# Block mixing with the data stationary: keys and values mixed straight into transposed form, Sinkhorn without matmuls, scores of two heads at once

## The chip, the cores and the metric

The kernel runs on one core of one Trainium2 chip. The metric is the device time of one execution in microseconds (us), as a median over several runs. Most executions of one kernel agree within a fraction of a per cent.

The engines are named as in the profile. PE is TensorE (matmuls), PEld its weight loads, DVE is VectorE, ACT is ScalarE, POOL is GpSimd and SP is SyncE. SBUF is the on-chip memory from which the engines work. PSUM is the small memory into which TensorE writes, and from which VectorE and ScalarE copy the results out. Such a copy is called an eviction here.

## The reference

There are 4 batches, 8 heads, 768 tokens in 8 blocks of 96, and a head width of 64. Each head has an 8x8 matrix, which is normalised and then mixes the blocks of keys and values. Attention is local to a block. A token mix and a two-layer channel MLP follow.

```python
P = sort_net                                   # [4, 8, 8, 8]
for _ in range(5):                             # Sinkhorn
    P = np.exp(P - np.max(P, axis=-1, keepdims=True))
    P = P / (np.sum(P, axis=-1, keepdims=True) + 1e-09)
    P = P / (np.sum(P, axis=-2, keepdims=True) + 1e-09)
k_sorted = np.einsum('bhij,bhjcd->bhicd', P, k_b)   # k_b: [4, 8, 8 blocks, 96, 64]
v_sorted = np.einsum('bhij,bhjcd->bhicd', P, v_b)
scores = scale * q_b @ k_sorted.T                   # per block, 96 x 96
x = softmax(scores) @ v_sorted                      # then [4, 768, 512]
a1 = alpha1 * x + beta1
u  = x + lam * np.einsum('ts,bsd->btd', w_tok, a1)  # token mix, 768 x 768
a2 = alpha2 * u + beta2
out = u + lam * (np.maximum(a2 @ w_ch1, 0.0) @ w_ch2)   # 512 -> 2048 -> 512
```

## The kernel before

Mixing works on a pair of batches: 2 batches x 8 heads x 8 blocks are 128 rows, so one 128x128 block-diagonal matrix (`bigP2`) mixes them all. The matrix is stationary and the data are moving, so each result comes out as it went in: rows are blocks, and a block's 96 tokens lie along the row. Attention needs tokens on the partitions. The kernel gets there by writing the mixed rows to DRAM and reading them back.

```python
def do_mix(bp):
    for (src, kv) in ((k, 0), (v, 1)):
        # ... for half, for chn: load raw [128, 1024]
        for n in range(2):
            mx = psb([128, 512], FT, name="mix_ps")
            nc.tensor.matmul(mx[:], bigP2[bp][:], raw[:, n * 512:(n + 1) * 512], start=True, stop=True)
            nc.scalar.copy(sort_t[:, chn * 1024 + n * 512: chn * 1024 + (n + 1) * 512], mx[:])
        # ... then, per batch, the DRAM scratch
        nc.sync.dma_start(kvscr[bb][:, :, kv, :]...[:, half * 48:(half + 1) * 48, :], sort_t[...]...)

def head_stage1(b, h):                              # one head at a time
    # ... the Q tile, and the tile kvn with its ones
    nc.sync.dma_start(kvn[:, :, 0:2 * D], kvscr[b, h].rearrange("(i t) kv d -> t i (kv d)", t=BLK))
    # ... the PSUM tile kTps
    for i in range(NB):                             # K once more, turned on TensorE
        nc.tensor.transpose(kTps[:, i * BLK:(i + 1) * BLK], kvn[:, i, 0:D], ident16[0:BLK, 0:BLK])
    # ... the SBUF tile kTs
    nc.vector.tensor_copy(kTs[:], kTps[:])
    # ... eight 96x96 score matmuls, exp on ScalarE
```

Other parts that the change touches are these. Sinkhorn uses ones-vector matmuls for its sums. 32 small DMAs put its result into `bigP2`. The attention output goes through a second DRAM scratch (`xscr`), to come back in token tiles. The affine of the channel MLP is folded into W1, with 64 bias matmuls. TensorE does not run the parts strictly in the order in which the program writes them: in this trace matmuls of the channel MLP (line 255) stand between those of an attention (lines 150, 163 and 181).

The softmax here doesn't subtract the row's maximum and nothing guards it: scores larger than these inputs give would overflow.

## Time and profile before

| | before |
|---|---|
| time, median | 434.53 us (434.02 to 438.99, the 3 runs before the prediction) |
| TensorE busy | 330.0 us of 433.1 |
| DRAM scratch and other small moves (queue q1) | 77,880 packets, 12.60 MB |
| from 180 us on | TensorE busy nearly all of every stretch |

The first view is the page of the profile. A strip has 40 slices of the span, and each digit is the busy share in tenths. A group line reads: source line, engine, operation, output<-input, shapes, count, then busy us and mean ns of one, then how long the engine stood idle just before them and on what.

```profile
span 433.1 us, 5706 instructions
...
PE   2474204432588342999999999999999999999996
...
ACT  1040004332334110177720066740046780048600
...
q1 hardware_dynamic: 77880, 12.60, 17.3%
...
L127 ACT CAST sort<-mix_ps 128x512 f16<-128x512 f32 x48 | 24.8, 605 | 63.4 <-DMA kvscr<-sort 22.0
...
L150 PE MATMUL kT_ps<-ident_71,kvn 96*64 96x96 f16 x256 | 19.4, 227 | 1.7 <-DMA kvn<-kvscr 1.7
```

The second view is the table by stretches of the same kernel: the stretch, its length, busy us of PE, PEld, DVE, ACT and POOL, then the clock granted to TensorE, the DMA share and GB/s.

```profile
60.00:80.00 20.00, 7.14 (x14) 1.17 (x14) 0.00 (x0) 6.25 (x12) 7.48 (x15) 1.00 0.62 90
80.00:100.00 20.00, 6.94 (x13) 1.08 (x14) 0.00 (x0) 6.07 (x12) 3.70 (x7) 1.00 1.17 183
...
180.00:200.00 20.00, 19.76 (x205) 13.55 (x203) 8.42 (x28) 13.50 (x29) 0.00 (x0) 1.00 0.18 41
200.00:220.00 20.00, 20.00 (x174) 12.81 (x174) 6.37 (x25) 15.18 (x28) 3.28 (x4) 1.00 0.85 174
```

There are two regimes. Up to 180 us every engine is mostly idle: in the mixing (60 to 100 us) TensorE works a third of the time, and ScalarE, which evicts 128x512 tiles at 605 ns each, waits 22.0 us in all for its tile to be stored to the scratch. From 180 us on TensorE is the bound. The change aims at the first regime, and takes some TensorE work (the 256 K transposes of line 150) out of the second.

### The profile page before, as it was taken

To read this page: it belongs to the slowest core of one execution; us is meant where nothing else is said; L and a number is where in the kernel's file an instruction comes from. 1 tells how busy PE (TensorE), PEld (TensorE's weight loads), DVE (VectorE), ACT (ScalarE), POOL (GpSimd) and SP (SyncE) were. 2 spreads that over 40 slices of the span, in tenths; PEclk is the share of its full clock that TensorE was granted. 3 is DMA by queue.
4 is the path that set the end of the run, shared out by engine and by line. 5 is a ranking of instruction groups with operands and counts; after the bars stand their busy time and mean duration, and the time that the engine had idled before them with its cause. 6 is when DMAs were issued, how large, how long until landed. Compare 5 with 4: busy or idle time off the path is not lost.

```text
span 433.1 us, 5706 instructions
## 1 busy us (share of the span) xinstructions
PE 330.0 (76%) x2264; PEld 182.0 (42%) x2264; DVE 156.4 (36%) x375; ACT 147.6 (34%) x290; POOL 64.8 (15%) x109
## 2 busy tenths in 40 slices
PE   2474204432588342999999999999999999999996
PEld 1331000000275230466644566654456654456542
DVE  0459830000144324545363435419335517330011
ACT  1040004332334110177720066740046780048600
POOL 6737142121100240000300030030010000000000
PEclk9999999999999996899999999999999999999999
DMA  9999706999967999413942173491221153300012
GB/s 87 157 211 202 89 0 101 183 173 158 200 121 115 188 66 233 68 38 76 180 124 87 40 45 74 112 209 50 98 18 38 38 144 108 113 2 0 2 73 74
DMA packets 120658, 44.30 MB, mean 102 GB/s; under 512 B 104824, under 2 KB 110712, under 8 KB 120632
## 3 DMA queue, kind: packets, MB, share of 16 engines
q0 software_dynamic: 35984, 21.90, 34.9%
q1 hardware_dynamic: 77880, 12.60, 17.3%
q10 hardware_dynamic: 6768, 9.44, 6.5%
q8 instruction: 18, 0.29, 0.3%
q14 instruction: 8, 0.07, 0.0%
HBM read 39.86 MB, written 15.73 MB: 128 GB/s over the span
## 4 chain that ended last, share of the span: by engine, by line
issue 45%; PE 27%; DMA 17%; DVE 5%; POOL 3%; ACTq 2%; ACT 0%; POOLq 0%; DVEq 0%
PE ch_ps L268 10%; PE h_ps L255 9%; DMA raw<-in_k_dram 4%; DMA raw<-in_v_dram 4%; DMA W1p_96<-in_moe_w_ch_dram 3%; DMA qn_1204<-in_q_dram 2%; ACTq L345 2%; PE tok_ps L226 2%; DVE jsum_r L324 2%; DMA qn_128<-in_q_dram 1%; DMA qn_172<-in_q_dram 1%; PE qT_ps L102 1%; PE x_ps L181 1%; PE mix_ps L122 1%; PE sc_ps L163 1%
## 5 line engine op out<-in xcount | busy, mean ns | idle before, releaser
L127 ACT CAST sort<-mix_ps 128x512 f16<-128x512 f32 x48 | 24.8, 605 | 63.4 <-DMA kvscr<-sort 22.0
L154 DVE COPY kTs<-kT_ps 64x768 f16<-64x768 f16 x32 | 17.4, 544 | 67.3 <-PE kT_ps L150 67.3
L169 ACT ACTIVATE ET<-sc_ps 96x384 f16<-96x384 f32 x64 | 27.6, 481 | 16.6 <-PE sc_ps L163 15.0
L122 PE MATMUL mix_ps<-raw,bigP_0_115 128*128 128x512 f16 x24 | 12.5, 603 | 24.8 <-DMA bigP_1_117<-PT_378 8.5
L107 DVE COPY qT<-qT_ps 64x768 f16<-64x768 f16 x32 | 16.7, 546 | 33.4 <-PE qT_ps L102 32.9
L188 DVE RECIPROCAL recip<-x_ps 96x4 f32<-96x4 f32 x64 | 11.1, 177 | 41.4 <-PE x_ps L181 40.3
L122 PE MATMUL mix_ps<-raw,bigP_1_117 128*128 128x512 f16 x24 | 12.5, 606 | 15.6 <-DMA raw<-in_k_dram 8.2
L163 PE MATMUL sc_ps<-qT,kTs 64*96 64x96 f16 x256 | 20.3, 227 | 3.2 <-DVE kvn L143 2.6
L163 PEld LDWEIGHTS <-kTs 64*96 64x96 f16 x256 | 16.1, 137 | 14.2 <-issue 5.7
L150 PE MATMUL kT_ps<-ident_71,kvn 96*64 96x96 f16 x256 | 19.4, 227 | 1.7 <-DMA kvn<-kvscr 1.7
L181 PE MATMUL x_ps<-kvn,ET 96*96 96x65 f16 x256 | 20.3, 227 | 0.0
L275 DVE TENSOR_TENSOR ost<-ch_ps,x_3_3331 128x512 f32<-128x512 f32 x6 | 4.1, 691 | 40.8 <-PE ch_ps L268 40.8
L181 PEld LDWEIGHTS <-ET 96*96 96x96 f16 x256 | 16.5, 140 | 2.5 <-issue 0.2
L122 PEld LDWEIGHTS <-bigP_0_115 128*128 128x128 f16 x24 | 2.0, 111 | 35.2 <-DMA raw<-in_v_dram 11.6
L150 PEld LDWEIGHTS <-kvn 96*64 96x64 f16 x256 | 14.8, 123 | 4.6 <-DMA kvn<-kvscr 2.2
L255 PEld LDWEIGHTS <-W1p_94 128*128 128x128 bf16 x128 | 12.6, 98 | 8.1
L255 PEld LDWEIGHTS <-W1p_96 128*128 128x128 bf16 x128 | 12.5, 98 | 7.9
L255 PEld LDWEIGHTS <-W1p_95 128*128 128x128 bf16 x128 | 12.5, 98 | 7.6
L255 PEld LDWEIGHTS <-W1p_97 128*128 128x128 bf16 x128 | 12.6, 98 | 7.0
L117 POOL DMA_DIRECT2D raw<-in_v_dram x12 | 6.4, 530 | 43.7 <-PE kT_ps L150 19.4
L321 PE MATMUL csp<-PT_216,ones_262 8*1 8x256 f32 x10 | 5.0, 604 | 8.7 <-ACT PT_216 L319 8.7
L122 PEld LDWEIGHTS <-bigP_1_117 128*128 128x128 f16 x24 | 2.1, 110 | 22.4 <-DMA raw<-in_k_dram 10.7
(490 smaller groups left out, 792.9 us busy)
## 6 DMA issues: line engine op xcount, KB each, us to landing
kvscr<-sort SPq DMA_DIRECT2D x16, 384.0 KB
kvn<-kvscr SPq DMA_DIRECT2D x32, 192.0 KB
out_dram<-ost ACTq DMA_DIRECT2D x24, 256.0 KB
raw<-in_k_dram POOLq DMA_DIRECT2D x12, 256.0 KB, 5.8
raw<-in_v_dram POOLq DMA_DIRECT2D x12, 256.0 KB, 5.8
x_0_950<-xscr POOLq DMA_DIRECT2D x1, 1536.0 KB, 7.6
x_1_1597<-xscr POOLq DMA_DIRECT2D x1, 1536.0 KB, 7.2
x_2_2464<-xscr POOLq DMA_DIRECT2D x1, 1536.0 KB, 8.7
```

What stands on the lines that cost most here:

```text
L107: nc.vector.tensor_copy(qT[:], qTps[:])
L122: nc.tensor.matmul(mx[:], bigP2[bp][:], raw[:, n * 512:(n + 1) * 512], start=True, stop=True,)
L127: nc.scalar.copy(sort_t[:, chn * 1024 + n * 512: chn * 1024 + (n + 1) * 512], mx[:])
L150: nc.tensor.transpose(kTps[:, i * BLK:(i + 1) * BLK], kvn[:, i, 0:D], ident16[0:BLK, 0:BLK])
L154: nc.vector.tensor_copy(kTs[:], kTps[:])
L163: nc.tensor.matmul(scps[:, ii * BLK:(ii + 1) * BLK], kTs[:, i * BLK:(i + 1) * BLK], qT[:, i * BLK:(i + 1) * BLK], start=True, stop=True,)
L169: nc.scalar.activation(ET[:, g * 4 * BLK:(g + 1) * 4 * BLK], scps[:], AF.Exp, scale=scale)
L181: nc.tensor.matmul(xps[:, ii * GRP: ii * GRP + D + 1], ET[:, i * BLK:(i + 1) * BLK], kvn[:, i, D:2 * D + 1], start=True, stop=True,)
L188: nc.vector.reciprocal(recip[:, g * 4:(g + 1) * 4], xg[:, :, D])
L226: nc.tensor.matmul(tps[:], w_tokT[ks][:, kt * 128:(kt + 1) * 128], a1p[:, ks, :], start=(ks == 0), stop=(ks == NT - 1),)
L255: nc.tensor.matmul(hps[:], W1p[ci][:, m * 128:(m + 1) * 128], a2T[ci][:, tci * 384:(tci + 1) * 384], start=(ci == 0), stop=(ci == CT - 1),)
L268: nc.tensor.matmul(cps[:], hT[m][:, kt * 128:(kt + 1) * 128], W2p[m][:], start=(m == 0), stop=(m == HT - 1),)
```

## The change

The intent is to turn the matmuls of the mixing round. The data become the stationary operand and the mixing matrix the moving one, so that the result comes out transposed: V with tokens on the partitions, K with the head dimension on the partitions, as attention wants them. The DRAM scratch and the K transposes go. What remains is to put each PSUM result into the SBUF tile that attention reads, and this is done by the evictions themselves.

```diff
+    def mix_v(bp):
+        raw = raw_of[(bp, 1)][:].rearrange("p (t d) -> p t d", d=D)
+        rhs = bigP[bp][:].rearrange("p g i -> p (g i)")
+        for d0 in range(0, D, 4):
+            vps = psa([BLK, 4, 128], FT, "v_ps")
+            for dd in range(4):
+                nc.tensor.matmul(vps[:, dd, :], raw[:, :, d0 + dd], rhs, start=True, stop=True)
+            dst = Vs[0][:, :, d0:d0 + 4].rearrange("p c d -> p d c")
+            if (d0 // 4) % 2 == 0:
+                nc.vector.tensor_copy(dst, vps[:])
+            else:
+                nc.scalar.copy(dst, vps[:])
+
+    def mix_k(bp):
+        raw = raw_of[(bp, 0)]
+        rhs = bigP[bp][:].rearrange("p g i -> p (g i)")
+        kT = att.tile([128, 8, NB, BLK], F16, name="kT", tag="kT", bufs=1)
+        kT_of[bp] = kT
+        for t0 in range(0, BLK, 8):
+            kps = psa([128, 4, 128], FT, "k_ps")
+            for tp in range(4):
+                c0 = (t0 + 2 * tp) * D
+                nc.tensor.matmul(kps[:, tp, :], raw[:, c0:c0 + 128], rhs, start=True, stop=True)
+            for par in range(2):
+                for h2 in range(2):
+                    src = kps[par * 64:(par + 1) * 64, :, h2 * 64:(h2 + 1) * 64]
+                    dst = kT[h2 * 64:(h2 + 1) * 64, :, :, t0 + par:t0 + 8:2].rearrange(
+                        "p g i t -> p t (g i)"
+                    )
+                    if par == 0:
+                        nc.vector.tensor_copy(dst, src)
+                    else:
+                        nc.scalar.copy(dst, src)
 ... cut: two heads share one score matmul, with zero-padded Q
+                nc.tensor.matmul(
+                    sps[:, ii, :, :].rearrange("p a t -> p (a t)"),
+                    kT[:, b2 * 4 + h4, 2 * g + ii, :],
+                    qb[:, 2 * g + ii, :, :].rearrange("p a t -> p (a t)"),
+                    start=True, stop=True,
+                )
 ... cut: Sinkhorn as [32, 8, 8] on VectorE, with one matmul per pair that spreads it over the
 ... partitions; u cast to fp16 on GpSimd; the affine applied in the eviction of u's transpose,
 ... so no bias matmuls; the scratch for the attention output replaced by three partition
 ... copies on GpSimd, with the token rows permuted to fit
+    mix_v(0)
+    mix_k(0)
+    emit_q(0)
+    emit_attention(0)
+    prep_wtok()
+    prep_affine()
 ... cut: loads of the second pair
     moe_a(0)
+    prep_w2()
+    emit_q(1)
     emit_attention(1)
     moe_b(0)
     moe_a(1)
+    mix_v(1)
+    mix_k(1)
+    emit_q(2)
     emit_attention(2)
 ... cut: the rest of the order
```

Two strings in this diff matter later: `"p c d -> p d c"` and `"p g i t -> p t (g i)"`. They fix the order in which an eviction walks over its destination. In both, the innermost index is the column of the mixing matrix, and neighbouring values of it lie 132 bytes apart in the V tile and 192 bytes apart in the K tile (66 and 96 elements of two bytes).

## The prediction

> **What bounds the kernel now.** Two regimes, from the stretch table (20 us windows). From 180 us to the end TensorE is busy 94 to 100% of every window but the last: a PE-bound tail of 253 us. From 0 to 180 us it works 83 us. There the timeline shows, in turn: weight and Q loads (to 43 us, DMA full near 200 GB/s of destination bytes); a Sinkhorn chain of five 8 us steps, interleaved with weight scaling, ending at 58.7 us; 32 tiny DMAs for the mixing matrix (to 67 us); block mixing held up by its DRAM round trip (ScalarE waits 22 us for the scratch store); one cold attention (115 to 144 us, 3.07 us per head); a second round trip for its output.
>
> **What the change does.**
> Removes: the DRAM scratch (12.6 MB on q1 in 77,880 packets), the tiny DMAs, 256 K transposes, fp32 transposes of u, 64 bias matmuls, Sinkhorn's matmuls and 1.75 us reciprocals.
> PE per batch, by spacing in the tail: h 20.8, ch 20.7, tok 7.8, uT 3.3 us; attention 240 short matmuls at 60 ns, 14.4. After (estimates from those spacings): uT 1.5; attention 24x60 + 32x80 + 64x60 ns = 7.9; mixing 112 matmuls at 60 ns = 6.7 per pair.
> Adds: transposing evictions from PSUM, per pair on ScalarE and VectorE each 8 of 96x512 (0.6 us, as the 605 ns cast) and 24 of 64x256 (0.36 us, estimate): 13 us each. Zero-padded Q. GpSimd copies (u to fp16, partition shift), about 0.77 us per 512 columns (estimate from the Trainium skill, "GPSIMD Engine Reference", Performance versus the Vector engine; no run here shows it).
>
> **Startup, as I expect it.** Loads stay on one queue at 205 GB/s: V to 10 us, K 17.5, Q 25.5, w_tok 32, W1 45, W2 55. Sinkhorn ends near 13 us, but the identity is built only after the Q issues, which wait for K (at most eight outstanding), so mixing starts near 22 us. Token-weight transposes stand inside K mixing in PE's order, so PE waits for w_tok until 33 us; mixing ends at 44. VectorE's order puts W2 scaling ahead of the padded-Q copies, so the first attention waits for W2, about 54 us; VectorE-bound, it ends at 71; then x shift, affine, token mix; h starts about 93 us.
> Then PE has 222 us left (4x41.5 + 3x9.3 + 6.7 + attention 5.5+15.8), stalls I put at 18 us (7 in the second mixing, ScalarE 22 us of work against PE's 15; the rest in attentions and GpSimd hops), and a 5 us tail.
>
> **Predicted: 338 us, 8 in 10 between 322 and 358.** Faster by over 2%: 0.97; within: 0.02; slower: 0.01.
>
> **What would show it.** PE starved before 90 us and over 90% busy after; W2's landing releasing VectorE just before the first padded-Q copy; PE waiting for w_tok inside K mixing; a PE dip in the second mixing with ScalarE near full; PE busy sum about 50 us lower; no scratch traffic.
>
> **What would make it wrong.** Strided weight reads for V slowing LDWEIGHTS; PE at its slow clock in the sparse start ("TensorE: Matmul & The Clock Gate", Back-to-back issue gap: N/1.2 ns cold, N/2.4 warm; this trace agrees, eight short transposes take 0.85 us in the sparse stage, 0.5 in the dense one); scattered evictions slower than dense ones; GpSimd copies far slower; another DMA order; stalls far from 18 us.

## The result, and the profile after

| | before | after |
|---|---|---|
| time, median | 434.27 us (432.73 to 438.99, 4 runs) | 404.87 us (404.10 to 405.15, 4 runs) |
| TensorE busy | 330.0 us | 313.3 us |
| VectorE busy | 156.4 us | 241.1 us |
| ScalarE busy | 147.6 us | 214.0 us |
| queue q1 | 77,880 packets, 12.60 MB | 5,040 packets, 6.31 MB |

The ratio of after to before is 0.9312, with a 95% interval from 0.9263 to 0.9362. A ratio is always computed as the mean time of one kernel's fast runs over that of the other's in the same rounds, so it is not quite the ratio of the medians that are quoted.

The kernel is faster, as predicted, but by 30 us instead of 96, and the time lies far outside the predicted range. This is its page, in the same form as above; the line that begins with "PE ch_ps" is the chain of work that ended last, by engine and line.

```profile
span 403.4 us, 4958 instructions
...
PE   0055895259489999995744449999999999989995
...
DVE  5169999997996812268999964842478512400021
ACT  2049799993029750029999997710087700077400
...
PEclk9999999999699999995555557999999999989999
...
q1 hardware_dynamic: 5040, 6.31, 5.7%
...
PE ch_ps L388 21%; PE h_ps L379 19%; ACT kT L228 15%; PE tok_ps L353 6%; ACT Vs_215 L207 5%; DVE Vs_215 L205 4%; PE sc_ps L262 4%; PE x_ps L280 3%; DMA raw_72<-in_v_dram 3%; DMA qn<-in_q_dram 2%; ACT a2T L367 2%; ACT et L269 1%; DVE a1p L346 1%; PE v_ps L202 1%; ACT w_tokT L327 1%
...
L228 ACT CAST kT<-k_ps 64x256 f16<-64x256 f32 x48 | 68.8, 1432 | 3.8 <-DVE kT L226 3.0
L226 DVE CAST kT<-k_ps 64x256 f16<-64x256 f32 x48 | 69.1, 1439 | 1.0
...
L207 ACT CAST Vs_215<-v_ps 96x512 f16<-96x512 f32 x16 | 36.8, 2743 | 16.1 <-PE v_ps L202 16.1
...
L205 DVE CAST Vs_215<-v_ps 96x512 f16<-96x512 f32 x16 | 37.2, 2607 | 3.9 <-PE v_ps L202 3.9
```

This is its table by stretches, with the columns as before.

```profile
60.00:80.00 20.00, 7.88 (x48) 5.20 (x48) 19.70 (x16) 19.72 (x16) 3.27 (x4) 1.00 0.29 19
...
180.00:200.00 20.00, 14.18 (x83) 11.98 (x83) 17.40 (x9) 19.86 (x11) 0.00 (x0) 0.56 0.00 1
200.00:220.00 20.00, 10.20 (x47) 5.28 (x45) 19.68 (x15) 18.88 (x17) 0.00 (x0) 0.50 0.00 0
220.00:240.00 20.00, 9.25 (x47) 5.22 (x46) 18.18 (x18) 19.67 (x18) 6.21 (x8) 0.50 0.46 30
```

The group lines say where the time is. A K eviction, predicted at 360 ns, takes 1432 to 1439 ns, and a V eviction, predicted at 600 ns, takes 2607 to 2743 ns. The dense 128x512 eviction of the kernel before, on ScalarE and with as many elements per partition as V's, took 605 ns. In the chain of work that ended last, the evictions of lines 228, 207 and 205 alone hold 24%. In the stretches from 180 to 240 us, which is the second mixing, VectorE and ScalarE are nearly full, TensorE works 46 to 71% of the time, and its granted clock is 0.56 and then 0.50. Before, TensorE was full from 180 us on. So the change freed the start of its DRAM waits, but moved the bound of the mixing to the two evicting engines, and it opened a new hole in what had been a solid TensorE tail. TensorE has other work in that hole, and still waits. These are two of its groups from 177 to 241 us:

```profile
L379 PE MATMUL h_ps<-a2T,W1p 128*128 128x384 bf16 x46 | 18.6, 521 | 0.0
...
L218 PE MATMUL k_ps<-bigP_205,raw_785 128*128 128x128 f16 x48 | 6.7, 303 | 14.3 <-ACT kT L228 12.7 <-DVE Vs_215 L205 0.9 <-ACT Vs_215 L207 0.6
```

Line 379 is the channel MLP, so 46 of its matmuls stand among those of the mixing. Before the K matmuls TensorE stood idle for 14.3 us, mostly waiting for an eviction of line 228 on ScalarE.

The miss can be read as two terms. The first matmul of the channel MLP (line 379) was predicted at 93 us and starts at 121.2 us, which is 28 us late: the first mixing, predicted to end at 44 us, runs from 24.3 to 86 us. From there to the end, 404.87 - 121.2 = 283.7 us pass, where the prediction had 338 - 93 = 245: another 39 us, in the part that holds the second mixing. Together that is 67 us, the whole of the miss.

### The profile page after: what moved, and what is told of

The parts are those of the page before. It is cut to its first block, busy times and chain, and to the rows that moved or that the text cites. A ratio compares the mean times of both kernels' runs of the same rounds, so it can differ in the third digit from the quotient of the medians.

```text
span 403.4 us, 4958 instructions
## 1 busy us (share of the span) xinstructions
PE 313.3 (78%) x1914; PEld 190.4 (47%) x1914; DVE 241.1 (60%) x378; ACT 214.0 (53%) x284; POOL 84.5 (21%) x116
## 3 DMA queue, kind: packets, MB, share of 16 engines
q1 hardware_dynamic: 5040, 6.31, 5.7%
## 4 chain that ended last, share of the span: by engine, by line
PE 56%; ACT 24%; DVE 8%; DMA 5%; issue 4%; POOL 1%; POOLq 0%; ACTq 0%
PE ch_ps L388 21%; PE h_ps L379 19%; ACT kT L228 15%; PE tok_ps L353 6%; ACT Vs_215 L207 5%; DVE Vs_215 L205 4%; PE sc_ps L262 4%; PE x_ps L280 3%; DMA raw_72<-in_v_dram 3%; DMA qn<-in_q_dram 2%; ACT a2T L367 2%; ACT et L269 1%; DVE a1p L346 1%; PE v_ps L202 1%; ACT w_tokT L327 1%
## 5 line engine op out<-in xcount | busy, mean ns | idle before, releaser
L379 PE MATMUL h_ps<-a2T,W1p 128*128 128x384 bf16 x512 | 104.8, 351 | 1.5 <-ACT a2T L367 1.2
L228 ACT CAST kT<-k_ps 64x256 f16<-64x256 f32 x48 | 68.8, 1432 | 3.8 <-DVE kT L226 3.0
L226 DVE CAST kT<-k_ps 64x256 f16<-64x256 f32 x48 | 69.1, 1439 | 1.0
L379 PEld LDWEIGHTS <-W1p 128*128 128x128 bf16 x512 | 52.9, 106 | 33.0 <-issue 7.5
L90 POOL DMA_DIRECT2D qn<-in_q_dram x32 | 26.3, 832 | 114.5 <-PE q_ps L239 101.0
L207 ACT CAST Vs_215<-v_ps 96x512 f16<-96x512 f32 x16 | 36.8, 2743 | 16.1 <-PE v_ps L202 16.1
L269 ACT ACTIVATE et<-sc_ps 96x384 f16<-96x384 f32 x64 | 27.3, 493 | 27.3 <-PE sc_ps L262 24.9
L205 DVE CAST Vs_215<-v_ps 96x512 f16<-96x512 f32 x16 | 37.2, 2607 | 3.9 <-PE v_ps L202 3.9
L353 PE MATMUL tok_ps<-a1p,w_tokT 128*128 128x512 bf16 x144 | 34.4, 397 | 6.5 <-DVE a1p L346 6.1
L280 PEld LDWEIGHTS <-et 96*96 96x96 f16 x256 | 19.3, 143 | 2.7
L280 PE MATMUL x_ps<-Vs_215,et 96*96 96x65 f16 x256 | 20.0, 222 | 0.1
L218 PE MATMUL k_ps<-bigP_205,raw_785 128*128 128x128 f16 x48 | 6.7, 303 | 14.3 <-ACT kT L228 12.7
## 6 DMA issues: line engine op xcount, KB each, us to landing
W1p<-in_moe_w_ch_dram POOLq DMA_DIRECT2D x4, 512.0 KB, 10.8
```

Of the source, the lines that this page charges most:

```text
L90: nc.gpsimd.dma_start(qn[:, :, h2, :], q[b, 2 * h4 + h2].rearrange("(kt p) d -> p kt d", p=128))
L205: nc.vector.tensor_copy(dst, vps[:])
L207: nc.scalar.copy(dst, vps[:])
L226: nc.vector.tensor_copy(dst, src)
L228: nc.scalar.copy(dst, src)
L269: nc.scalar.activation(et[:], sps[:], AF.Exp, scale=scale)
```

## The experiments

The runs were taken in three sessions, each with its own runs of before: order_both, dense_both, one_engine and probe (before at 434.93 us), then order_k, order_v, v_stationary and late_w2 (433.92), then ident_first and both_early (435.64). A difference between runs of two sessions is therefore good to about 2 us.

**Theory A, scatter.** An eviction that writes each two-byte value far from the last one costs several times a dense one, on the writing side, whichever engine does it.

**Rival B, contention.** VectorE and ScalarE evict at the same time, from PSUM and into the same tile, and slow each other.

**Rival C, the read.** The layout of the source in PSUM is what costs. This rival is also a warning about the remedy: whoever turns the loop round reads PSUM in steps of 512 bytes.

### order_both: the same evictions, walked in another order

The same values go to the same places; only the order of the walk is turned, so that four nearby values of the destination are written in succession (2 bytes apart in V, 4 bytes apart in K). Nothing else changes.

```diff
-            dst = Vs[0][:, :, d0:d0 + 4].rearrange("p c d -> p d c")
+            dst = Vs[0][:, :, d0:d0 + 4]
-                nc.vector.tensor_copy(dst, vps[:])
+                nc.vector.tensor_copy(dst, vps[:].rearrange("p d c -> p c d"))
 ... and the same for the ScalarE copy; for K:
-                    src = kps[par * 64:(par + 1) * 64, :, h2 * 64:(h2 + 1) * 64]
+                    src = kps[par * 64:(par + 1) * 64, :, h2 * 64:(h2 + 1) * 64].rearrange("p t c -> p c t")
-                        "p g i t -> p t (g i)"
+                        "p g i t -> p (g i) t"
```

> Same tiles, same addresses, same values and a right result; only the order in which each K and V eviction walks its elements is turned, so that writes go in runs of four neighbours (V: 8 bytes in a row; K: four elements 4 bytes apart) and PSUM is read with a step of 512 bytes. Theory A (scatter: a copy pays for each 2-byte write that lands far from the one before): K copies fall from 1.43 us to 0.4 to 0.7 us, V copies from 2.3 to 0.6 to 1.1 us, the kernel to about 345 us (335 to 360). Theory B (the two engines hinder each other when both write one tile at once): copies stay at 1.43 and 2.3 us, kernel within 2% of 405. Theory C (reading PSUM is what is slow): copies the same or slower, kernel 405 or more.

It was correct, at 347.13 us (345.34 to 348.11), ratio to before 0.7964 [0.7917, 0.8011]. These are the lines of its groups, by shape:

```profile
L228 ACT CAST kT<-k_ps 64x256 f16<-64x256 f32 x48 | 22.8, 475 | 4.7 <-DVE kT L226 4.0
L226 DVE CAST kT<-k_ps 64x256 f16<-64x256 f32 x48 | 22.7, 472 | 11.5 <-PE k_ps L218 10.6
...
L202 PEld LDWEIGHTS <-raw 128*96 128x96 f16 x128 | 22.0, 255 | 0.9 <-issue 0.7
L280 PE MATMUL x_ps<-Vs,et 96*96 96x65 f16 x256 | 19.7, 220 | 0.3 <-DVE qbd L247 0.2
L262 PE MATMUL sc_ps<-qbd,kT 128*96 128x192 f16 x128 | 19.3, 275 | 6.8 <-issue 5.9 <-ACT kT L228 0.4 <-DVE qbd L247 0.3
...
L205 DVE CAST Vs<-v_ps 96x512 f16<-96x512 f32 x16 | 11.0, 688 | 12.0 <-PE v_ps L202 12.0
```

A K eviction fell from 1439 to 472 ns and a V eviction on VectorE from 2607 to 688 ns (595 ns on ScalarE), and the kernel fell by 58 us, into the predicted range. On VectorE the evictions now wait for TensorE (10.6 and 12.0 us). The first matmul of the channel MLP starts at 99.6 us, and 247.5 us pass from there to the end, against the predicted 93 and 245. Theory A stands, and rival C in its strong form falls: the read that steps 512 bytes is the faster variant.

The first mixing still ends only at 58.2 us. What holds it now are two of TensorE's groups from 34.4 to 58.2 us, the transposes of the token weights, which stand between the K matmuls:

```profile
L319 PE MATMUL wtok_ps<-identbf,wt 128*96 128x128 bf16 x36 | 11.4, 317 | 0.0
L323 PE MATMUL wtok_ps<-identbf,wt 128*32 128x128 bf16 x36 | 9.9, 274 | 0.0
```

TensorE is busy for 23.7 of these 23.8 us, while the K evictions need 11.4 us on each engine.

### order_k and order_v: one at a time

```diff
 order_k: only the K lines of the edit above
 order_v: only the V lines of the edit above
```

> Only the K evictions walk in the turned order, V as in the changed kernel. Right result. If the scattered writes are the whole cause, and add up: K copies 0.48 us instead of 1.43, 24 of them per mixing on each engine, so about 23 us less per mixing and 44 us (36 to 48) less for the kernel, 361 us. If the two kinds of copies hide each other (a fix of one alone is worth little), 390 us or more.

> Only the V evictions walk in the turned order. Right result. Eight copies of 2.3 us per engine and mixing become 0.6 us, but then TensorE's own 64 V matmuls (10.6 us measured in the run with both turned) bind that part, so about 8 us less per mixing and 15 us (8 to 20) less for the kernel, 390 us; together with the K run this should give back the 58 us of the run with both.

K alone gave 366.56 us (366.51 to 366.87), ratio 0.8451 [0.8410, 0.8493]. V alone gave 387.19 us (386.67 to 387.53), ratio 0.8924 [0.8886, 0.8961]. Against the 404.87 us of after these are gains of 38 and 18 us, together 56, where both at once gave 58. So the two parts add up, and K is the larger.

### one_engine: all evictions of the mixing on VectorE

```diff
-                nc.scalar.copy(dst, vps[:])
+                nc.vector.tensor_copy(dst, vps[:])
-                        nc.scalar.copy(dst, src)
+                        nc.vector.tensor_copy(dst, src)
```

> The order of the changed kernel, but all K and V evictions on VectorE and none on ScalarE. Right result. Theory A: each copy keeps its 1.43 and 2.3 us, and with twice as many on one engine each mixing grows by about 50 us: kernel about 500 us (470 to 520). Theory B: each copy falls to half or less (0.7 and 1.2 us or under) and the kernel stays within 5% of 405.

It was correct, at 483.55 us (one run, of unknown state), within the 470 to 520 us of theory A. The time isn't the point; the duration of one eviction with no ScalarE beside it is. These are two lines of its groups:

```profile
L226 DVE CAST kT<-k_ps 64x256 f16<-64x256 f32 x48 | 69.0, 1438 | 1.0
...
L207 DVE CAST Vs<-v_ps 96x512 f16<-96x512 f32 x16 | 42.3, 2644 | 0.0
```

1438 ns against 1439, and 2644 against 2607: an eviction is as slow alone as in company. Rival B falls.

### probe: the copy by itself, at eight steps

After the kernel of after, copies of one 64x256 PSUM tile were added into the K tile, which is free by then, four of each form on each engine. The destination's innermost step is 1, 2, 4, 8, 16, 32, 64 and 96 elements of two bytes. Further forms read PSUM at a 512-byte step and write densely, write runs of four values at a 132-byte step, and copy fp16 values from SBUF.

```diff
+        d_8 = kf[0:64, 0:512].rearrange("p (c s) -> p s c", s=8)[:, 0:4, :]
+        copy(d_8, src)          # four times; the other steps likewise
+        dd = kf[0:64, 0:256].rearrange("p (c t) -> p c t", t=4)
+        copy(dd, src.rearrange("p t c -> p c t"))   # read at a step, write dense
```

> The changed kernel with a measuring tail that nothing depends on: copies of one 64x256 fp32 PSUM tile into fp16, four of each form, on VectorE and then on ScalarE, with steps of 1, 2, 4, 8, 16, 32, 64 and 96 elements between successive writes; then reads of PSUM at a step of 512 bytes with dense writes; the same with writes in runs of four at a step of 132 bytes; and copies from SBUF to a step of 96 and to a step of 1. Theory A: about 0.35 us dense, 1.4 us at 96 on both engines, growing somewhere in between, from SBUF as from PSUM; strided PSUM reads with dense writes near 0.35 us. Theory B: 0.35 us at every step, since only one engine copies at a time. Theory C: the strided PSUM reads cost 1 us or more, the write steps nothing.

It was correct. Its 442.27 us, a single run, mean nothing, because the copies were added at the end. These are lines of its groups: lines 438, 450, 456 and 480 are steps of 1, 4, 8 and 96 elements, line 485 is the read at a step with a dense write, and lines 495 and 499 are copies from SBUF to a step of 96 elements and to a dense row.

```profile
L480 ACT CAST kT<-probe_ps 64x256 f16<-64x256 f32 x1 | 1.4, 1432 | 0.0
...
L480 DVE CAST kT<-probe_ps 64x256 f16<-64x256 f32 x1 | 1.4, 1429 | 0.0
...
L456 DVE CAST kT<-probe_ps 64x256 f16<-64x256 f32 x1 | 1.3, 1296 | 0.0
...
L450 DVE CAST kT<-probe_ps 64x256 f16<-64x256 f32 x1 | 0.7, 718 | 0.0
...
L438 DVE CAST kT<-probe_ps 64x256 f16<-64x256 f32 x1 | 0.4, 417 | 0.3 <-PE probe_ps L428 0.3
...
L485 DVE CAST kT<-probe_ps 64x256 f16<-64x256 f32 x1 | 0.4, 417 | 0.0
...
L495 DVE COPY kT<-x 64x256 f16<-64x256 f16 x1 | 0.8, 798 | 0.0
...
L499 DVE COPY kT<-x 64x256 f16<-64x256 f16 x1 | 0.2, 219 | 0.0
```

| step of the write, bytes | 2 | 4 | 8 | 16 | 32 | 64 | 128 | 192 |
|---|---|---|---|---|---|---|---|---|
| VectorE, ns | 417 | 436 | 720 | 1295 | 1236 | 1279 | 1287 | 1429 |
| ScalarE, ns | 368 | 426 | 724 | 1293 | 1241 | 1277 | 1291 | 1432 |

The table has the median of the four copies of each form, all of them from PSUM. A step of 4 bytes is nearly free, 8 bytes cost 1.7 times the dense copy on VectorE and 16 bytes 3.1 times, and from there to 192 bytes it changes by no more than 11%. The jump is at the same place on both engines, so its place belongs to where the values go and not to one engine. The 192-byte step, the kernel's own, gives 1429 ns on VectorE and 1432 on ScalarE, where the kernel's K evictions have medians of 1430 and 1433. The read of PSUM at a 512-byte step costs nothing: 417 ns against 417. Runs of four values at a 132-byte step, the turned walk of V, took 416 ns.

The size of the cost is not fixed by the destination alone. The expectation was that a copy from SBUF would behave as one from PSUM. On ScalarE it did (1468 ns at 192 bytes, 404 dense). On VectorE the same write took 799 ns, against 219 dense: still 3.6 times, but 580 ns more instead of 1012. The source's memory and its type (fp16 for fp32) changed together here, so which of them matters was not tested.

The Trainium skill, in "SBUF — State Buffer", section "Specifications (TRN2)", says this in its row on cachelines: they are of 16 bytes, and a line needs "≥2 hits per line for full bandwidth; each cross to a new line pays a penalty". The probe agrees in where the cost saturates, at 16 bytes, and gives the size that the page does not, for a copy from PSUM on VectorE: (1295 - 417) / 256 = 3.4 ns more per value. At a step of 8 bytes, which is two values in a line, the penalty is a third of that but not yet gone, so there the measurement is stricter than the page's two hits.

### dense_both: the tiles turned instead of the walk

If only the evictions count, one could lay the K and V tiles out so that the original walk is dense, and let TensorE read them at a step.

```diff
-    Vs = [const([BLK, 128, GRP], F16, f"Vs_{n}") for n in range(1)]
+    Vs = [const([BLK, GRP, 128], F16, f"Vs_{n}") for n in range(1)]
-        kT = att.tile([128, 8, NB, BLK], F16, name="kT", tag="kT", bufs=1)
+        kT = att.tile([128, BLK, 8, NB], F16, name="kT", tag="kT", bufs=1)
-                    kT[:, b2 * 4 + h4, 2 * g + ii, :],
+                    kT[:, :, b2 * 4 + h4, 2 * g + ii],
-                        Vs[0][:, col, 0:D + 1],
+                        Vs[0][:, 0:D + 1, col],
 ... and the evictions write these tiles densely
```

> The K and V tiles are laid out the other way round, so each eviction reads PSUM densely and writes rows of 64 or 128 neighbouring elements; the stride moves to TensorE, which now reads K as a strided stationary operand and V as a strided moving operand. Right result. Theory A: K copies about 0.36 us, V copies about 0.6 us, mixing no longer longer than 25 us each; kernel about 340 us (328 to 355) if TensorE takes strides freely; if TensorE pays for them too, the score and value matmuls get longer than their 60 to 80 ns spacing and the gain is smaller. Theory B: copies stay above 1.2 and 2 us, since both engines still write one tile at once; kernel near 405. Theory C: the same as B.

It was correct, at 361.12 us (359.90 to 362.44), ratio 0.8300 [0.8248, 0.8351]: 44 us better than after, but 14 us behind order_both. These are lines of its groups:

```profile
L280 PE MATMUL x_ps<-Vs,et 96*96 96x65 f16 x256 | 33.6, 287 | 0.0
...
L262 PE MATMUL sc_ps<-qbd,kT 128*96 128x192 f16 x128 | 25.7, 327 | 6.0 <-issue 5.6 <-DVE qbd L247 0.2
L262 PEld LDWEIGHTS <-kT 128*96 128x96 f16 x128 | 23.8, 251 | 7.8 <-issue 5.8 <-ACT kT L228 0.5 <-DVE qbd L247 0.4
```

The evictions are quicker than in order_both (K 417 ns on VectorE and 368 on ScalarE), as theory A asks. But the matmuls that read V as moving data take 33.6 us against 19.7, and those that read K as weights 25.7 us against 19.3. Together that is 20 us of TensorE, the engine that bounds most of this kernel. So a stride on TensorE's side was dearer than one on the reading side of the eviction, though it was still 44 us cheaper than the scattered writes of after.

### v_stationary: does TensorE also pay when it loads V's weights at a step?

The prediction had named this as a risk. In mix_v the stationary operand is one column of the head dimension, that is, 96 values 128 bytes apart. Here 96 neighbouring values are loaded instead, which gives a wrong result; the base is order_both.

```diff
-                nc.tensor.matmul(vps[:, dd, :], raw[:, :, d0 + dd], rhs, start=True, stop=True)
+                nc.tensor.matmul(vps[:, dd, :],
+                    raw_of[(bp, 1)][:, (d0 + dd) * BLK:(d0 + dd + 1) * BLK], rhs, start=True, stop=True)
```

> On top of both evictions turned: the V matmuls take 96 neighbouring columns as their stationary operand instead of columns 128 bytes apart. The result is wrong on purpose. If strided reads of the stationary operand slow TensorE, the spacing of V matmuls falls from 0.166 us (first mixing) and 0.138 (second) to about 0.11 and 0.06 as for K, that is 4 and 5 us, and the kernel from 347 to about 340 us (337 to 344). If the spacing comes from something else (the wait for PSUM buffers), it stays and so does the time.

Its time is 335.75 us (333.42 to 336.75), ratio 0.7731 [0.7688, 0.7775], which is 11 us below order_both by the medians and 10 by the ratios, and just below the expected 337 to 344; the relative error is 1.43. This is the weight load in its groups:

```profile
L202 PEld LDWEIGHTS <-raw 128*96 128x96 f16 x128 | 10.0, 139 | 2.1 <-issue 1.4
```

The load of the same 96 columns takes 139 ns, against 255 ns at a step. In the first mixing the 64 matmuls of V begin between 24.1 and 29.3 us, where in order_both they begin between 24.0 and 34.3 us, so their spacing is 5.2 / 63 = 0.083 us against 10.3 / 63 = 0.163 us. In the second mixing the V matmuls begin within 7.5 us instead of 12.3. The risk was real, and worth 10 to 11 us once the evictions are quick.

### late_w2: what holds the first attention once the mixing is short

The prediction said that VectorE's order puts the scaling of W2 ahead of the padded-Q copies. Here the scaling goes to GpSimd, after the first token mix; the first line makes it wait for that without changing a value.

```diff
+        nc.vector.scalar_tensor_tensor(out=lamB[:], in0=u_of[0][NT - 1][:], scalar=0.0,
+            in1=lamB[:], op0=ALU.mult, op1=ALU.add)
-            nc.vector.tensor_tensor(W2p[:, m, :], W2p[:, m, :], lamB[:], ALU.mult)
+            nc.gpsimd.tensor_tensor(W2p[:, m, :], W2p[:, m, :], lamB[:], ALU.mult)
```

> On top of both evictions turned: W2 is scaled on GpSimd after the first token mix instead of on VectorE ahead of the padded-Q copies. Right result. If the first attention waits behind that scaling, as the prediction said (5 us of it stood ahead of the first padded-Q copy in the run with both turned, and some 7 more further on before the affine), the start of the dense stage comes 6 to 10 us earlier and the kernel at 339 us (335 to 343). If the mixing still hides it, within 1% of 347.

It was correct, at 338.08 us (338.05 to 338.17), ratio 0.7793 [0.7761, 0.7825]: 9 us below order_both by the medians, 7 by the ratios. The first padded-Q copy starts at 59.5 instead of 62.8 us and the channel MLP at 94.9 instead of 99.6 us. So the order named in the prediction is real, and costs 3 us at the first copy and 5 us by the channel MLP. The other 4 us are gained after that point. There TensorE has 229 us of work left instead of 233, and the same 12 us of idle time: by the trace, more of the second attention's matmuls (28 of line 280 and 12 of line 262) came before that point. That the scaling caused this shift was not tested.

### ident_first and both_early: is the late identity on the path?

In after, the two identity matrices are built by GpSimd behind the Q loads, which wait for K. In order_both, VectorE's first mask (line 133) waits 10.8 us for the identity, and mixing starts at 24 us. Here the identity is built before the loads, alone and together with late_w2.

```diff
+    ident16 = const([128, 128], F16, "ident16")
+    make_identity(nc, ident16)
+    identbf = const([128, 128], BF, "identbf")
+    make_identity(nc, identbf)
     # ... then the loads
     load_q(0)
-    ident16 = ...   (the same four lines)
```

> The copies with the order turned, plus one move: the two identity matrices that the mixing needs are built before the loads are issued, instead of after the Q issues that wait for K. Theory: with the order turned the first mixing starts at 24 us only because the identity comes late, so it now starts near 13 us with V and ends earlier by about 8 us; but the first attention waits for the W2 scaling anyway (it begins at 58 us, when W2 has landed), so the time stays at 347 us, within 1%. Rival: the start of the mixing is what the first attention hangs on, and the time falls by 8 us, to 339.

> The copies with the order turned, the identity built first, and the W2 scaling moved to GpSimd after the first token mix. Theory: with W2 out of the way (338 us so far) the first mixing is on the critical path, so the earlier identity is now worth about 8 us: 330 us. Rival: token weights, which land near 32 us and whose transposes stand inside the K mixing in TensorE's order, hold the mixing whatever its start: 336 to 338 us, no gain.

ident_first gave 339.36 us (338.47 to 339.57), ratio 0.7781 [0.7742, 0.7820]. The theory said 347, and was wrong; the rival was right. The mixing starts at 13.3 us and the last K eviction starts at 36.9 us. The theory had taken it that the W2 scaling, which starts at 58.0 us in order_both, starts when W2 has landed. This is the view of the tile W2p in ident_first, up to 110 us:

```profile
L335 DVE TENSOR_TENSOR W2p<-W2p,lamB x16: 677/685/1523, 50.2 to 85.5; 128x512 bf16<-128x512 bf16 x16
...
its engine sat idle before it (us, times) until:
  DMA W2p<-in_moe_w_ch_dram: 12.5, 2
```

VectorE has now nothing to do and sits idle for 12.5 us until W2 lands at 50.2 us. In order_both it came to the scaling only after the mixing, at 58.0 us: it was the end of the mixing that counted there, and the landing counts only here. The first scores start at 56.7 instead of 64.0 us, and these 7 us are most of the gain. The move did more than bring the start forward: TensorE's instructions come in another order too. In order_both the token-weight transposes stand between the K matmuls, and in ident_first most of them come after these, so that the K evictions run from 24.5 to 37.4 us instead of from 35.1 to 58.2.

both_early gave 329.69 us (329.08 to 330.54), ratio 0.7566 [0.7532, 0.7601]. The theory said 330. It is the best version found, correct, and better than both given kernels: 105 us below before and 75 us below after. This is its page:

```profile
span 327.3 us, 4965 instructions
...
PE   0496999978899999998779999999999999799994
...
DVE  5659641799634712546958851367870125000111
```

The hole of the second mixing is nearly closed: from 60 us on no slice of TensorE is below 7 but the last.

## Why the prediction was wrong

Seen by where the channel MLP starts, the experiments line up. The columns are the start of the first score matmul, the start of the first matmul of line 379 (line 384 in the kernels with late W2), and the time.

| kernel | scores, us | channel MLP, us | time, us |
|---|---|---|---|
| predicted | 54 | 93 | 338 |
| after | 85.9 | 121.2 | 404.87 |
| order_v | 77.2 | 112.8 | 387.19 |
| order_k | 73.2 | 108.7 | 366.56 |
| order_both | 64.0 | 99.6 | 347.13 |
| both_early | 51.6 | 86.1 | 329.69 |

- **The failed step** is one term: "transposing evictions from PSUM, per pair on ScalarE and VectorE each 8 of 96x512 (0.6 us, as the 605 ns cast) and 24 of 64x256 (0.36 us, estimate): 13 us each". In the first mixing the trace has 18.4 us for V and 34.4 us for K on each of the two engines, 53 us instead of 13. The 605 ns came from a dense eviction of the kernel before, and was carried over to one that scatters. With the order of the walk turned and nothing else, 347.13 us lies within the predicted 322 to 358. So this term alone took the time outside its range.
- That order_both then comes within 10 us of the predicted 338 is partly luck. Its first mixing ends at 58.2 us instead of 44. The V loads at a step hold TensorE about 5 us longer, and the token-weight transposes, which the prediction named only as a wait for the weights, keep it busy for 21 us between the K matmuls. What held the first attention was the end of this mixing and not the landing of W2. The scores start 10 us late, but the channel MLP follows them after 35.6 us instead of the predicted 39.
- The prediction listed "scattered evictions slower than dense ones" among what would make it wrong, but priced them as dense ones in its sum. The Trainium skill's row on cachelines ("SBUF — State Buffer", "Specifications (TRN2)") tells where to look. The string that sets the walk was in the diff, with 192 bytes between successive writes.
- Because the evictions bound the mixing, "a PE dip in the second mixing with ScalarE near full" came true in kind (ScalarE 19.86 of 20 us), but lasted 64 us, from 177 to 241 us, instead of about 22. TensorE also had matmuls of the channel MLP there (18.6 us), but stood idle for 27 us of this time, 26 of them waiting for evictions.
- "PE busy sum about 50 us lower" was 17 lower. Part of that goes with the clock, which was granted at 0.50 to 0.56 through the second mixing: there a matmul of line 379 took 521 ns, where its median in the whole kernel is 326. These matmuls alone, which are the same in both, have 104.8 us busy in after and 95.1 in order_both. In order_both the sum is 294.9 us, 35 lower. Most of what remains are the V loads at a step: in v_stationary, without them, it is 282.0 us, 48 lower.
- "Strided weight reads for V slowing LDWEIGHTS" was right: 255 ns against 139, worth 10 to 11 us once the evictions were quick.
- Right as well were: no scratch traffic (5,040 packets on q1, which are the output and small loads); the identity that comes after the Q issues and starts the mixing near 22 us (24.3); and VectorE's order, which puts W2 ahead of the padded Q. In after W2's landing itself is hidden behind the long mixing, and it shows only in ident_first. TensorE did not wait for the token weights: their transposes stand in the K mixing, as said, but the weights had landed, and what they cost was their own time.
- The GpSimd estimate of 0.77 us per 512 columns, from the Trainium skill's "GPSIMD Engine Reference", section "Performance versus the Vector engine", was on the safe side: the u cast took 0.63 us (24 of them, in order_both).
- The tail was right: from the start of the channel MLP to the end, 247.5 us in order_both against the predicted 245.

## What to carry to other kernels

When a copy turns a layout round, read from its access pattern how many bytes lie between two successive writes: with two-byte values evicted from PSUM a 4-byte step was nearly free and a 16-byte step tripled the copy, and which loop is innermost decides between them. A duration taken from a dense copy may be carried over only to another dense copy. If something has to be strided, let the engine that evicts from PSUM do it on its reading side: that cost nothing on either engine in the probe, while both strided writes and strided TensorE operands cost tens of microseconds.

## What the Trainium skill lacked or had wrong

- "SBUF — State Buffer", "Specifications (TRN2)": the cacheline row has a size of 16 bytes that fits the place where the cost saturates, but no price. Measured for 256 two-byte values per partition on VectorE, from PSUM: 417 ns dense, 720 at 8 bytes, 1295 at 16 bytes, 1429 at 192; from SBUF 219 dense and 799 at 192. At 8 bytes, two values in a line, it was not yet at full rate.
- "VectorE: DVE Perf Modes", section "Mode 1× (REGULAR) — the baseline", says of the fallback mode that "it makes no assumptions. fp32, weird strides, PSUM operands — all work", and counts one result per cycle. They work, but not at one rate: the same copy from PSUM took 417 or 1429 ns by the step of its destination alone.
- "PSUM — Partial Sum Buffer", "Specifications (TRN2)", warns that any non-contiguous pattern in PSUM slows matmuls significantly. No page found gives a figure for an engine that reads it: a 512-byte step cost nothing on either (417 against 417 ns on VectorE, 366 against 368 on ScalarE).
- "TensorE: Matmul & The Clock Gate", section "LDWEIGHTS (loading the stationary operand)", makes the time depend on the number of columns alone. With 96 columns it was 139 ns for neighbouring values and 255 ns for values 128 bytes apart. The page has no price for a strided moving operand either: the x matmuls took 33.6 us instead of 19.7 with one.
